# Tokens 0 to 255 of x turned on TensorE instead of by the DMA queue, at the start of a fused attention and token-mixer kernel

## The chip, the cores and the metric

The kernel runs on one core of one Trainium2 chip. The metric is the time of one execution on the device in microseconds (us), the median over several runs; lower is better. The profile shows one such execution: when each instruction of the engines TensorE (PE, with its weight loads as PEld), VectorE (DVE), ScalarE (ACT), GpSimd (POOL) and of the DMA-issuing queues of SyncE and ScalarE (SPq, ACTq) began, how long it took and what released it.

## The reference

The input `x` has 2048 tokens of 448 features. Two branches read it, and a gate for each token mixes them:

```
g = sigmoid((x * gate_w).sum(-1, keepdims=True))
a = _A_ref(x, wq, wk, wv, wo, beta)        # attention in 4 segments of 512 tokens, 16 heads of 28
b = _B_ref(x, w1, b1, w2, b2)              # layernorm, then an MLP over the token axis (2048 -> 1792 -> 2048)
return g * a + (1 - g) * b
```

In `_A_ref`, `q = x @ wq`, `k = x @ wk` and `v = x @ wv` are formed first. Each segment then has causal softmax attention inside it and a read of a running memory `M`, which sums `phi(k)^T v` of the earlier segments; the two are blended by `sigmoid(beta)` and projected by `wo`. `_B_ref` contracts the token axis, so it needs `x` with tokens on the partitions; the projections of `_A_ref` contract the feature axis, so they need `x` turned, with features on the partitions. The change is about how the first half of the first segment gets turned.

## The kernel before

**Two copies of x.** `xh` holds `x` as rows, 16 tiles of 128 tokens, loaded by `load_x` (L533). `xT` holds it turned: four feature chunks `c` of 128 features (chunk 3 begins at feature 320 and overlaps chunk 2, and the matmuls on it use half of its rows) by 2048 tokens. `transpose_x(tc)` (L548) fills the 512 tokens of segment `tc` with two DMAs that transpose while they move: `dtx{tc}_0` for chunks 0 to 2 and `dtx{tc}_1` for chunk 3.

**The start.** SyncE issues, in this order, the two transposing DMAs of segment 0, the loads of `wk` and `wq`, the two of segment 1, and then three of the four loads of `xh`. ScalarE meanwhile issues the gate vector, the four parts of `wv` (L538 and, for the last part, L542), the last part of `wk` and two biases; only then does it load its function table and begin to compute. TensorE runs ten matmuls on constants (`warm`, L664), a small transposition of the gate vector (`gtr`, L879), and then the value projection of token tiles 0 to 3.

**The value projection** of a tile `t` is split by what it needs. `pra{t}` is chunk 0, `prb{t}` chunk 1, `prt{t}` chunk 2 or 3 over all 128 rows. `lot0` and `lot2` take the remaining 64-row halves of chunk 2 or 3 for two tiles at once, side by side in the array. The turned tokens are the weights of these matmuls, `wv` with the gate vector as column 449 is what streams through. Every projection matmul goes through the helper `mm`, so all of them have line 296. After them come the key projections (`pra0_1`, `pra0_2`, `pra0_0`, a `lok` pair, and so on), which need `wk` spread out to 32 columns a head by VectorE's copies `padk`, `padx` (L675); the pair `lok0_2` also needs the first two such copies of `wq` (`padq0`, `padq1`). `cpv` (L857 on ScalarE, L859 on VectorE) moves a value tile out of PSUM, `gt` (L860) its gate column, `cpk` (L773, L775) a key group. `prt7` is the first matmul that reads segment 1 of `xT`. From there on the program goes through scores (L1015), exponentials (L1024, ScalarE), value products (L1045) and the two token-mixer matmuls (again L296), closely interleaved.

**What sets the order.** `ORDER` is a table with a line-up of operation names for each engine; an entry such as `pra0@5` also gives the PSUM bank. `Sched.plan` puts each engine's instructions out in exactly that order, and `finalize` adds the semaphore waits that the recorded reads and writes require. An engine executes its list in order: whatever stands behind a waiting instruction waits as well. The resources `R_xT[tc][k]` say which part of `xT` an operation reads; before the change there are two for each segment, one for each transposing DMA.

Of the kernel before, what the change touches and what calls it, by code (L numbers as in the profile page):

```python
# [324 lines left out]
u1-15 u2-10*4 u3-5*2 u4-0@4 u3-7*2 sc1_1 u5-0@6*2 u2-14 u5-2*2 u2-15 u3-9*6 u5-4 u3-15 u4-1*5 u5-5*2 pv1@7 u4-6*2
sc1_2 u4-8 u5-7*5 u4-9*4 u5-12 pv0@5 u5-13 sc1_3 u4-13*3 u6-0@7*3 u7-0@5 u6-3 u5-14 u6-4*2 u5-15 u6-6 sc1_4 u6-7 u7-1
u6-8*4 u7-2*2 u6-12 u7-4*3 u6-13*3 sc2_0 u7-7*7 pv2@6 u7-14*2 sc2_1 mst0@4 u8-0@6*2 prq2_1@7 prq2_0@5 loq2_0 sc2_2
u8-2*4 prq2_2@4 u8-6*4 prq2_2h@7 loq2_2 mem1 u8-10*2 u9-0@4 u8-12 u9-1*8 u8-13*2 u11-0@5 sc2_3 u9-9*3 pv3@7 u9-12
u8-15 u9-13*2 u11-1 u9-15 u11-2*4 sc2_4 u10-0@7*3 u11-6*6 u13-0@4 u10-3 pv4@6 sc3_0 u10-4*12 u11-12 u13-1 sc3_1
u13-2*3 u11-13*2 u13-5*2 pv5@6 u11-15 prt9@7 u13-7*4 sc3_2 lot8@6 u13-11*2 u12-0@5*5 prt8 u13-13*3 u12-5 sc3_3  # L330
lot10@67 u12-6*3 prt11 u12-9*7 prt10 sc3_4 mst1@7 prk3_1@4 pv6@5 prk3_0@7 lok3_0 sc4_0 prq3_1@6 prq3_0@7 wo0@5 loq3_0
lw0@4 sc4_1 wo1 pv7@6 prk3_2@5 wo3@7 lok3_2@4 lw2@6 sc4_2 wo2 prx3_3 y0-0@5*5 mem2 y0-5*9 prq3_2h@6 prq3_2@4 loq3_2
sc4_3 y1-0@7*7 y2-0@4 y1-7 y2-1 sc4_4 y2-2*2 y1-8 y3-0@6*3 pv8@5 y2-4 y1-9 sc5_0 y2-5*2 y3-3*3 y1-10 y3-6*5 sc5_1
y3-11*3 y1-11*3 y2-7 wo4@5 sc5_2 lw4@7 wo5 y2-8 pv9@6 y2-9*2 sc5_3 y2-11*3 y5-0@5*7 sc5_4 lw6@64 y5-7 pv10@7 wo7
# [4 lines left out]
lw12 lw14 y10-12 y11-12*2 y10-13 wo14 wo15 wo12 y12-0@4*2 wo13 y13-0@7*4 y15-0@5 y13-4*2 y14-0@6*2 y13-6*4 y12-2
y14-2*2 y13-10 y14-4 y12-3*2 y13-11 y12-5*3 y14-5 y15-1 y12-8*3 y14-6*3 y13-12*2 y12-11*3 y14-9*5 y15-2*12 y15-0#1@7  # L340
y15-1#1 y15-2#1 y15-3#1 y15-4#1 y15-5#1 y15-6#1 y15-7#1 y15-8#1 y15-9#1 y15-10#1 y15-11#1 y15-12#1 y15-13#1""",
    "ACT": """
ldwv0 ldgw ldwv1 ldwv2 ldwvb ldwkb ldb1 ldb2 cpv2 cpv0 gt0 gt2 cpv1 gt3 gt1 ek0_0 cpk0_1 cpk0_3 cpq0_3 ek0_1 cpv7 gt7
cpk1_3 cpq1_3 cpk1_2 cpv6 cpq0_2 gt6 cpq0_0 cpq0_2#1 cpq1_1 cpq1_2 cpq0_1 tb eq1_1 cpq1_2#1 exp0_0@2 cpk1_1 cpv5 cpv4
gt5 gt4 exp0_1@3 cpk2_2 cpk2_3 cpk2_1 exp0_2@4 cpk2_0 exp0_3@0 eq1_0 eq1_2 exp0_4@1 ek0_2 gsq0 exp1_0@5 gsq1 gvh1 gth0
exp1_1@6 gsq2 gth1 ek0_3 eq1_3 gsq3 gvh3 exp1_2@0 ek1_0 gth3 gth2 exp1_3@1 gsq4 gsq5 exp1_4@2 ek1_1 gth5 gth4 exp2_0@3
gsq6 gsq7 exp2_1@4 ek1_2 cpq2_1 exp2_2@5 ek1_3 cpq2_0 gth7 cpq2_2#1 gth6 eq2_2 eq2_0 exp2_3@6 gsq8 gsq9 eq2_1 gvh9
exp2_4@0 gth8 gth9 exp3_0@1 ek2_0 gsq10 ek2_1 gvh10 exp3_1@2 gsq11 gth10 exp3_2@3 cpv9 cpv8 gt8 gt9 gth11 exp3_3@4
cpv11 gsq13 gt11 gsq12 cpv10 exp3_4@0 gth12 gt10 cpk3_0 exp4_0@5 eq2_3 cpq3_1 cpq3_0 exp4_1@6 gth13 cpk3_2 exp4_2@7
cpk3_3 ag2 eq3_1 cpq3_3 ag3 ek2_2 exp4_3@1 ek2_3 exp4_4@2 eq3_0 exp5_0@0 eq3_2 exp5_1@3 exp5_2@4 exp5_3@5 ag5 exp5_4@6  # L350
eq3_3 exp6_0@1 ag6 exp6_1@2 exp6_2@7 cpv13 gt13 cpv12 gt12 exp6_3@0 gt15 gt14 exp6_4@3 exp7_0@4 ag9 exp7_1@5 exp7_2@6
exp7_3@1 exp7_4@2 ag11 ag15 ag14 ag12 ag13""",
# [39 lines left out]
def build_kernel(nc, X, WQ, WK, WV, WO, BETA, W1, B1, W2, B2, GW, OUT):  # L392
# [153 lines left out]
    def transpose_x(tc):  # L546
        for k, (c, n) in enumerate(((0, 3), (3, 1))):
            op("SP", lambda e, c=c, n=n: e.dma_start_transpose(  # L548
                xT[:, c : c + n, tc * 512 : tc * 512 + 512], x2[tc * 512 : tc * 512 + 512, C0[c] : C0[c] + 128 * n]),
               writes=[R_xT[tc][k]], name=f"dtx{tc}_{k}", dma=True, cost=1200 * n, nbytes=227000 * n, prio=(-3, -3, -1, 0)[tc])  # L550
# [217 lines left out]

    def do_k(tc, hg, t0=0, n=512):
        ks = kT[:, hg, tc * 512 + t0 : tc * 512 + t0 + n]  # L770

        def out(b):
            op("ACT", lambda e: e.activation(ks, bank(b)[:, 0:n], ACT.Copy),  # L773
               **buse(b), reads=[bres(b)], writes=[R_kTh[hg] if t0 else R_kT[hg][tc]], name=f"cpk{tc}_{hg}",
               cost=act_cost(n), prio=P_BASE, alt=("DVE", lambda e: e.tensor_copy(ks, bank(b)[:, 0:n]), dve_cost(n)))  # L775
# [603 lines left out]
```

## Time and profile before

| | |
|---|---|
| median of 3 runs | 170.5 us (170.43 to 170.8) |
| the profiled execution | 170.1 us, of which the profile's span is 168.3 us |
| instructions in the span | 4931 |
| busy: TensorE, VectorE, ScalarE, GpSimd | 164.0, 136.9, 130.4, 64.5 us |
| DMA | 25.44 MB, mean 151 GB/s |

Busy time is time in which at least one instruction of the engine is under way. Matmuls overlap in the array, so the ends of TensorE's rows are modelled and its busy share is no measure of its peak; its starts are recorded. In a row of the timeline the first number is the start, the second the time that the group covers, and the brackets at the end say how long the engine sat idle before it and what ended that. Times are us from the span's start.

### The profile page before, as it was taken

How to read it: one execution, taken by the hardware profiler on the slowest of the kernel's cores; microseconds unless marked ns; L12 is line 12 of the kernel's file. 1: busy time of each engine (PE TensorE's matmuls, PEld its weight loads, DVE VectorE, ACT ScalarE, POOL GpSimd, SP SyncE). 2: the span in 40 equal slices, each digit the busy share in tenths (PEclk: the TensorE clock that was granted, in tenths of full speed). 3: DMA queues.
4: the chain of work that ended last, by engine and by line, in shares of the span. 5: the costliest groups of instructions: out<-in, count | busy, mean ns of one | idle time of the engine just before them, and what ended most of it. 6: DMA issues, size and time to landing. Idle time of an engine off the chain costs nothing.

```text
span 168.3 us, 4931 instructions
## 1 busy us (share of the span) xinstructions
PE 164.0 (97%) x2017; PEld 77.6 (46%) x2017; DVE 136.9 (81%) x321; ACT 130.4 (77%) x164; POOL 64.5 (38%) x100
## 2 busy tenths in 40 slices
PE   8799999999999999999999999999999999999994
PEld 3234444444554544544453454444454444454553
DVE  0087999877989989999999999999999979695042
ACT  0359999999999997999999998988985798603200
POOL 5000245261442514142177356445838356541000
DMA  6999999886677955994338202328942129730302
GB/s 144 259 225 296 242 236 237 167 220 189 181 158 221 217 101 146 163 213 126 103 108 182 67 2 63 97 77 157 253 126 84 42 63 283 225 117 27 117 27 82
DMA packets 53974, 25.44 MB, mean 151 GB/s; under 512 B 18416, under 2 KB 53712, under 8 KB 53952
## 3 DMA queue, kind: packets, MB, share of 16 engines
q1 hardware_dynamic: 53160, 24.54, 59.2%
q10 hardware_dynamic: 792, 0.58, 1.6%
q8 instruction: 16, 0.26, 0.7%
q14 instruction: 6, 0.05, 0.1%
HBM read 18.82 MB, written 2.36 MB: 126 GB/s over the span
## 4 chain that ended last, share of the span: by engine, by line
PE 94%; DMA 3%; ACTq 1%; POOL 0%; issue 0%; DVE 0%; POOLq 0%
PE t L296 79%; PE t L1015 8%; PE t L1045 5%; DMA t<-in_A_wv_dram 3%; PE t L896 1%; PE t L1118 1%; ACTq L538 1%; ACTq L559 0%; DVE t L1251 0%; POOL t L557 0%; POOL t L633 0%; POOL t L600 0%; PE t L927 0%; POOL t L632 0%; POOL t L628 0%
## 5 line engine op out<-in xcount | busy, mean ns | idle before, releaser
L296 PE MATMUL t<-t 128*32 128x448 bf16 (+8 forms) x1252 | 140.5, 352 | 1.1 <-DMA t<-in_A_wv_dram 1.0
L296 PEld LDWEIGHTS t<-t 128*32 128x32 bf16 (+2 forms) x1252 | 63.0, 97 | 64.3 <-issue 14.2
L1024 ACT ACTIVATE t<-t 128x2048 bf16<-128x2048 f32 x40 | 75.2, 1879 | 6.8 <-PE t L1015 6.2
L1027 POOL TENSOR_SCALAR_AFFINE_SELECT t<-t 128x512 bf16<-128x512 bf16 x64 | 43.5, 691 | 42.5 <-ACT t L1024 39.6
L1082 POOL TENSOR_TENSOR t<-t 128x448 bf16<-128x448 f32 (+2 forms) x13 | 13.3, 1026 | 19.0 <-DVE t L1075 14.4
L1251 DVE SCALAR_TENSOR_TENSOR t<-t 128x448 bf16<-128x448 f32 (+2 forms) x17 | 10.7, 645 | 10.2 <-PE t L296 10.1
L1015 PE MATMUL t<-t 28*128 28x512 bf16 (+3 forms) x256 | 15.8, 301 | 0.0
L1059 DVE STREAM_TRANSPOSE t<-t 128x512 f32<-128x512 f32 x16 | 11.3, 706 | 2.9 <-PE t L1045 2.7
L965 POOL TENSOR_TENSOR t<-t 128x4 f32<-128x4 f32 x4 | 4.2, 1054 | 23.3 <-DVE t L963 21.6
L1157 ACT ACTIVATE t<-t 128x448 bf16<-128x448 f32 x10 | 7.0, 732 | 7.7 <-PE t L296 7.7
L1045 PE MATMUL t<-t 128*32 128x512 bf16 (+3 forms) x256 | 11.5, 299 | 0.0
L1101 DVE STREAM_TRANSPOSE t<-t 128x512 bf16<-128x512 bf16 x16 | 10.9, 690 | 0.0
L1015 PEld LDWEIGHTS t<-t 28*128 28x128 bf16 x256 | 4.4, 92 | 14.0 <-ACT t L1024 7.7
L956 DVE BATCH_NORM_STATS2 t<-t 128x6 f32<-128x448 bf16 x16 | 9.3, 610 | 1.1 <-DMA t<-in_A_x_dram 1.1
L857 ACT ACTIVATE t<-t 128x448 bf16<-128x448 f32 x13 | 6.8, 546 | 4.2 <-PE t L296 4.2
L1220 DVE SCALAR_TENSOR_TENSOR t<-t 128x448 f32<-128x448 f32 x14 | 9.2, 664 | 0.5 <-ACT t L1215 0.4
L1045 PEld LDWEIGHTS t<-t 128*32 128x32 bf16 x256 | 6.7, 97 | 5.3 <-issue 0.4
L1212 ACT ACTIVATE t<-t 128x448 f32<-128x448 f32 x14 | 8.8, 638 | 0.1
L818 ACT ACTIVATE t<-t 128x512 bf16<-128x512 bf16 x12 | 7.6, 635 | 1.4 <-DVE t L775 1.4
L847 DVE SCALAR_TENSOR_TENSOR t<-t 128x512 bf16<-128x512 bf16 x12 | 8.5, 712 | 0.1
L1075 DVE SCALAR_TENSOR_TENSOR t<-t 128x448 f32<-128x448 f32 x12 | 8.4, 698 | 0.0
L1225 DVE SCALAR_TENSOR_TENSOR t<-t 128x448 bf16<-128x448 f32 x14 | 8.4, 614 | 0.0
(76 smaller groups left out, 129.3 us busy)
## 6 DMA issues: line engine op xcount, KB each, us to landing
t<-in_B_w_dram SPq DMA_DIRECT2D x52, 256.0 KB, 3.4
t<-in_A_x_dram SPq DMA_DIRECT2D x4, 448.0 KB, 4.8
out_dram<-t SPq DMA_DIRECT2D x15, 112.0 KB, 1.9
t<-in_B_w_dram SPq DMA_DIRECT2D x8, 128.0 KB, 2.4
t<-in_A_wv_dram ACTq DMA_DIRECT2D x4, 112.0 KB, 4.1
t<-in_A_wq_dram SPq DMA_DIRECT2D x1, 336.0 KB, 5.1
spare_heads<-t SPq DMA_DIRECT2D x8, 32.0 KB
spare_heads<-t SPq DMA_DIRECT2D x16, 16.0 KB
```

The lines of the kernel that those rows point to most:

```text
L296: last = e.matmul(out[q], w[:, q], x, skip_group_check=True, **kw)
L956: op("DVE", lambda e: e.bn_stats(st6[:, t, :], xh[:, t, :]), reads=[R_x[t]], writes=[R_st6[t]], name=f"bns{t}", cost=512, prio=P_PROJ - 10 ...
L1015: last = e.matmul(bank(hl)[:, c0 : c0 + w], kT[r, hg, s * 512 + j * 128 : s * 512 + j * 128 + 128], qT[r, hg, s * 512 + 128 * j : s * 512 ...
L1024: exps.append(op("ACT", lambda e: e.activation(pslot(g), ps[:, 0:4, :], ACT.Exp, scale=SCALE), reads=R_bank[0:4], writes=[g.res], take=g, ...
L1027: op("POOL", lambda e, c0=c0: e.affine_select(pslot(g)[:, :, c0 : c0 + 128], pslot(g)[:, :, c0 : c0 + 128], pattern=[[0, 4], [1, 128]], co ...
L1045: last = e.matmul(bank(cb)[32 * ((hl + hg) % 4) : 32 * ((hl + hg) % 4) + 32, 128 * j : 512], vaug[:, 4 * s + j, 32 * h : 32 * h + 32], psl ...
L1059: dv(lambda e: e.transpose(tt[:, ia, :], bank(cb)[:, 0:512]), [bres(cb)], [R_tt[ia]], "ta", 630, use=(cb,))
L1082: return e.tensor_tensor(dst, part(n3[0]), part(n3[1]), op=ALU.add)
L1101: dv(lambda e: e.transpose(oT[:, hg, s * 512 : s * 512 + 512], o), [R_ob[hg]] + ([R_obx] if hg else []), qres(hg, s), "ot", 635)
L1212: op("ACT", lambda e: e.activation(gg[:, q, :], bank(b)[:, 0:D], ACT.Square, bias=b1s[:, ft : ft + 1], scale=math.sqrt(GC)), **buse(b), re ...
L1220: op("DVE", lambda e: e.scalar_tensor_tensor(gg[:, q, :], gg[:, q, :], 1.0, vh[:, q, :], op0=ALU.add, op1=ALU.mult), reads=[R_gg[q], R_vh[ ...
L1251: op("DVE", lambda e: e.scalar_tensor_tensor(outst[:, p, c0:c1], bank(b)[:, 0 : c1 - c0], omg[:, T : T + 1], ag(T)[:, c0:c1], op0=ALU.mult ...
```

## The change

`transpose_x(0)` turns tokens 256 to 511 only. Tokens 0 to 255 are loaded as rows, by `load_x("SP", 0, 2)`, which is issued behind `dtx0_0` and ahead of `dtx0_1`; the later load `ldx0` of four tiles becomes `ldx2` of two. A new function `turn_x` multiplies the loaded tiles with the identity: eight matmuls of 128 columns, four into PSUM bank 0 (`xt0_0`, chunks 0 and 1 of both tiles), four into bank 1 (`xt0_1`, chunks 2 and 3). One copy each brings a bank to `xT`: `cx0_0` on ScalarE and `cx0_1` on VectorE. `R_xT[0]` now has four entries, for the two copies and the two shorter DMAs, and `xres` picks those that a projection reads. In the order, value tiles 2 and 3 come ahead of 0 and 1; with them the PSUM banks 4 to 7 are given out in another rotation throughout. All other orders are kept.

```diff
@@ ORDER, the beginning of PE, ACT, DVE and SP
-warm gtr@4 warm2 pra0@5 pra1@6 pra2@7 pra3@4 prb3 prb2 prb0 prb1 lot2 lot0 prt1 prt3 prt2 prt0 pra0_1 pra0_2 pra0_0
+warm gtr@4 warm2 xt0_0 xt0_1 pra2@5 pra3@6 prb2 prb3 pra0@7 pra1@4 prb0 prb1 lot2 lot0 prt2 prt3 prt0 prt1 pra0_1
...
@@ build_kernel
-    R_xT = [R(f"xT{t}_", 2) for t in range(4)]
+    R_xT = [R(f"xT{t}_", 4 if t == 0 else 2) for t in range(4)]
+
+    def xres(tc, cs=range(NCT), halves=range(2)):
+        return [R_xT[0][k] for k in sorted({2 * p + c // (2 + p) for p in halves for c in cs})] if tc == 0 else \
+            [R_xT[tc][k] for k in sorted({c // 3 for c in cs})]
...
     def transpose_x(tc):
         for k, (c, n) in enumerate(((0, 3), (3, 1))):
-            op("SP", lambda e, c=c, n=n: e.dma_start_transpose(
-                xT[:, c : c + n, tc * 512 : tc * 512 + 512], x2[tc * 512 : tc * 512 + 512, C0[c] : C0[c] + 128 * n]),
-               writes=[R_xT[tc][k]], name=f"dtx{tc}_{k}", dma=True, cost=1200 * n, nbytes=227000 * n, prio=(-3, -3, -1, 0)[tc])
+            t0 = tc * 512 if tc else 256
+            op("SP", lambda e, c=c, n=n, t0=t0: e.dma_start_transpose(
+                xT[:, c : c + n, t0 : tc * 512 + 512], x2[t0 : tc * 512 + 512, C0[c] : C0[c] + 128 * n]),
+               writes=[R_xT[tc][k if tc else 2 + k]], name=f"dtx{tc}_{k}", dma=True, cost=1200 * n, nbytes=227000 * n, prio=(-3, -3, -1, 0)[tc])
 
     transpose_x(0)
+    load_x("SP", 0, 2)
...
-    load_x("SP", 0, 4)
+    load_x("SP", 2, 2)
...
+    def turn_x():
+        for k in range(2):
+
+            def fn(e, k=k):
+                for c in (2 * k, 2 * k + 1):
+                    for t in range(2):
+                        at = 256 * (c % 2) + 128 * t
+                        last = e.matmul(bank(k)[:, at : at + 128], xh[:, t, C0[c] : C0[c] + 128], ident[:, :],
+                                        start=True, stop=True, skip_group_check=True)
+                return last
+
+            op("PE", fn, reads=R_x[0:2] + [R_ident], writes=[R_bank[k]], name=f"xt0_{k}", mode="f",
+               cost=pe_cost(128, 128, 128, 128), prio=-1)
+
+            def ends(k=k):
+                return xT[:, 2 * k : 2 * k + 2, 0:256], bank(k).rearrange("p (c t) -> p c t", c=2)
+
+            op("ACT", lambda e, ends=ends: e.activation(*ends(), ACT.Copy), reads=[R_bank[k]], writes=[R_xT[0][k]],
+               name=f"cx0_{k}", cost=act_cost(512), prio=-1,
+               alt=("DVE", lambda e, ends=ends: e.tensor_copy(*ends()), dve_cost(512)))
...
+    turn_x()
```

What stands on the engines at the start is shown by three pairs of listings. Each row is a line of the source, an operation, what it writes and reads, and the semaphores that it waits for; `s_dma_u…` is the semaphore of one DMA.

TensorE before, from the first gate matmul to the key projections: `s_dma_u3`, `u4`, `u5`, `u6` are the four parts of `wv`, `u1` and `u2` the two transposing DMAs, `s_DVE` the gate column and later the spread-out `wk`.

```order
L879 MATMUL t<-t 128x3 [waits s_POOL,s_dma_u12]
L880 MATMUL t<-t 128x1
L664 MATMUL t<-const-bfloat16-1.0 128x512
L296 MATMUL t<-t 128x449 [waits s_DVE,s_dma_u3,s_dma_u1]
L296 MATMUL t<-t 128x449 x3
L296 MATMUL t<-t 128x449 [waits s_dma_u4]
L296 MATMUL t<-t 128x449 x3
L296 MATMUL t<-t 128x449 [waits s_dma_u6,s_dma_u5,s_dma_u2]
L296 MATMUL t<-t 128x449 x7
L296 MATMUL t<-t 128x512 [waits s_DVE]
```

TensorE after, the same stretch: `s_dma_u3` is now the load of the first two x tiles, the parts of `wv` are `u4` to `u7`, and `s_ACT` is the copy `cx0_0`.

```order
L671 MATMUL t<-const-bfloat16-1.0 128x512
L684 MATMUL t<-t 128x128 [waits s_dma_u3]
L684 MATMUL t<-t 128x128 x7
L296 MATMUL t<-t 128x449 [waits s_DVE,s_dma_u4,s_dma_u1]
L296 MATMUL t<-t 128x449
L296 MATMUL t<-t 128x449 [waits s_dma_u5]
L296 MATMUL t<-t 128x449
L296 MATMUL t<-t 128x449 [waits s_ACT]
L296 MATMUL t<-t 128x449 x3
L296 MATMUL t<-t 128x449 [waits s_dma_u7,s_dma_u6,s_dma_u2]
L296 MATMUL t<-t 128x449
L296 MATMUL t<-t 128x449 [waits s_DVE]
```

Eight turning matmuls stand ahead of all projections, and four of the eight matmuls on chunks 0 and 1 now stand behind a wait for ScalarE.

ScalarE after, its issues and its first computing instructions (before, the same list without the row of L694, and the table load belongs to `cpv2`):

```order
L547 DMA t<-in_A_wk_dram 128x448
L575 DMA t<-in_B_b_dram 14x128
L577 DMA t<-in_B_b_dram 16x128
L694 ACT_TABLE_LOAD
L694 ACTIVATE t<-t 128x2x256 [waits s_PE]
L886 ACTIVATE t<-t 128x16x28 [waits s_PE] x2
```

The copy `cx0_0` (L694) is the first computing instruction of ScalarE and stands behind eight DMA issues and the table load.

SyncE after, its first issues (before: the two transposing DMAs of 512 tokens, then the weights, then three loads of four tiles):

```order
L554 DMA_TRANSPOSE t<-in_A_x_dram 128x3x256
L538 DMA t<-in_A_x_dram 128x2x448
L554 DMA_TRANSPOSE t<-in_A_x_dram 128x1x256
L543 DMA t<-in_A_wk_dram 128x2x448
L543 DMA t<-in_A_wk_dram 128x448
L543 DMA t<-in_A_wq_dram 128x3x448
L547 DMA t<-in_A_wq_dram 128x448
L554 DMA_TRANSPOSE t<-in_A_x_dram 128x3x512
L554 DMA_TRANSPOSE t<-in_A_x_dram 128x1x512
L538 DMA t<-in_A_x_dram 128x2x448
L538 DMA t<-in_A_x_dram 128x4x448 x2
```

One more issue stands ahead of the weights on this queue, and the two transposing DMAs of segment 0 have half their tokens.

More of the change, by code (lines that the diff above doesn't have):

```diff
@@ L325 @@
[L325 to L334, printed above, removed]
@@ L340 @@
-y14-2*2 y13-10 y14-4 y12-3*2 y13-11 y12-5*3 y14-5 y15-1 y12-8*3 y14-6*3 y13-12*2 y12-11*3 y14-9*5 y15-2*12 y15-0#1@7
+warm gtr@4 warm2 xt0_0 xt0_1 pra2@5 pra3@6 prb2 prb3 pra0@7 pra1@4 prb0 prb1 lot2 lot0 prt2 prt3 prt0 prt1 pra0_1
+pra0_2 pra0_0 btr@7 lok0_0 lok0_2 prk0_0 prx0_3 prk0_2 prk0_1 prt7@5 prx1_3@6 prk1_2@4 lot6@7 lok1_2 loq0_0 loq0_2
+prq0_2 prq0_0 prt6 prq1_2@5 prq0_2h prq1_1@6 prq1_2h@4 loq1_0@7 loq1_2 prq0_1 prq1_0 prk1_1@6 sc0_0 lok1_0@5 lot4@74
+prk1_0 prt5 prt4 sc0_1 prk2_1@6 prx2_3@5 prk2_2@4 lok2_2 lok2_0@7 sc0_2 prk2_0 u1-0@4*5 u0-0@6 u1-5 u0-1*2 u2-0@5*3
@@ L350 @@
[L350 to L352 removed]
+ldwv0 ldgw ldwv1 ldwv2 ldwvb ldwkb ldb1 ldb2 cx0_0 cpv2 cpv0 gt0 gt2 cpv1 gt3 gt1 ek0_0 cpk0_1 cpk0_3 cpq0_3 ek0_1
+cpv7 gt7 cpk1_3 cpq1_3 cpk1_2 cpv6 cpq0_2 gt6 cpq0_0 cpq0_2#1 cpq1_1 cpq1_2 cpq0_1 tb eq1_1 cpq1_2#1 exp0_0@2 cpk1_1
@@ L353 @@
+exp4_2@7 cpk3_3 ag2 eq3_1 cpq3_3 ag3 ek2_2 exp4_3@1 ek2_3 exp4_4@2 eq3_0 exp5_0@0 eq3_2 exp5_1@3 exp5_2@4 exp5_3@5 ag5
+exp5_4@6 eq3_3 exp6_0@1 ag6 exp6_1@2 exp6_2@7 cpv13 gt13 cpv12 gt12 exp6_3@0 gt15 gt14 exp6_4@3 exp7_0@4 ag9 exp7_1@5
+exp7_2@6 exp7_3@1 exp7_4@2 ag11 ag15 ag14 ag12 ag13""",
     "DVE": """
-ob0 gw padk0 padx0 cpv3 padk1 padx1 padk2 padx2 padq0 padq1 b2c padq2 b1c padq3 cpk0_0 cpk0_2 mk0_0 bns3 bns1 bns0
-phk0_0 bns2 bna1 bna3 bna2 bns7 bns9 bna0 bns5 bns10 vpe0 bns11 bns6 bna9 cpq1_0 bna7 bns4 bna6 gcol0 bna5 bna4 vpe4
@@ L356 @@
-nmr0 bna10 bns8 ln1 b1h ln2 bna8 cpk1_0 b1s mk0_1 bns13 bna11 phk0_1 nmr4 bns15 ln0 bna15 omgh vpe8 ln3 ln4 gh ln5
-cpq2_3 bns12 bna12 bna13 bns14 ln6 mq1_1 bna14 nmr8 ln11 ln8 ln9 vpe12 ln10 ln7 omg0 nmr12 mg0 ln12 ln13 ln15 ln14
+ob0 gw cx0_1 padk0 padx0 cpv3 padk1 padx1 padk2 padx2 padq0 padq1 b2c padq2 b1c padq3 cpk0_0 cpk0_2 mk0_0 bns3 bns1
+bns0 phk0_0 bns2 bna1 bna3 bna2 bns7 bns9 bna0 bns5 bns10 vpe0 bns11 bns6 bna9 cpq1_0 bna7 bns4 bna6 gcol0 bna5 bna4
+vpe4 nmr0 bna10 bns8 ln1 b1h ln2 bna8 cpk1_0 b1s mk0_1 bns13 bna11 phk0_1 nmr4 bns15 ln0 bna15 omgh vpe8 ln3 ln4 gh
@@ L762, in proj_d @@
         ts = slice(tc * 512 + t0, tc * 512 + t0 + n)
-        need = R_xT[tc]
+        need = xres(tc)
         return dict(n=n, w=lambda c, rows: wqk[rows, c, 4 * G : 4 * G + 4, :].rearrange("p h j -> p (h j)"),
                     x=lambda c, rows: xT[rows, c, ts], need=need + R_w, use=xuse(tc).get("use", ()),
-                    by=lambda c: [need[c // 3]] + [R_w[k] for k in range(len(R_w)) if R_w[k] not in R_wkp or k % 3 == (0, 0, 1, 2)[c]],
+                    by=lambda c: xres(tc, (c,)) + [R_w[k] for k in range(len(R_w)) if R_w[k] not in R_wkp or k % 3 == (0, 0, 1, 2)[c]],
                     name=name + ("h" if t0 else ""), out=out)
@@ L778, in do_k @@
         if tc == 0:
-            P["first"] = [((0, 1), [R_xT[0][0], R_wkp[0], R_wkp[3]])]
+            P["first"] = [((0, 1), xres(0, (0, 1)) + [R_wkp[0], R_wkp[3]])]
         return P
@@ L861, in out, with rx @@
                **buse(b), reads=[bres(b)], writes=[R_gth[t]], name=f"gt{t}", cost=60, prio=P_BASE)
-        rx = R_xT[t // 4]
+        def rx(cs=range(NCT)):
+            return xres(t // 4, cs, (t % 4 // 2,))
         P = dict(n=D + 1, w=lambda c, rows: xT[rows, c, t * 128 : t * 128 + 128],
-                 x=lambda c, rows: wvx[rows, c, 0 : D + 1], need=rx + R_wv + [R_gw],
-                 by=lambda c: [rx[c // 3], R_wv[c], R_gw],
+                 x=lambda c, rows: wvx[rows, c, 0 : D + 1], need=rx() + R_wv + [R_gw],
+                 by=lambda c: rx((c,)) + [R_wv[c], R_gw],
                  use=xuse(t // 4).get("use", ()), name=f"prt{t}", out=out)
         if t < 4:
-            P["first"] = [((0,), [rx[0], R_wv[0], R_gw]), ((1,), [R_wv[1]])]
+            P["first"] = [((0,), rx((0,)) + [R_wv[0], R_gw]), ((1,), rx((1,)) + [R_wv[1]])]
         return P
```

55 lines of the change are left out of this document (31 added, 24 removed).

## The prediction

> **What bounds the kernel now.** I read the page first: the busy times, and the chain of work that ended last by engine.
>
> ```profile
> PE 164.0 (97%) x2017; PEld 77.6 (46%) x2017; DVE 136.9 (81%) x321; ACT 130.4 (77%) x164; POOL 64.5 (38%) x100
> PE 94%; DMA 3%; ACTq 1%; POOL 0%; issue 0%; DVE 0%; POOLq 0%
> ```
>
> TensorE carries 94% of the chain, DMA 3%. Where the DMA part lies is told by the chain in order of time (start, duration, what), and whether TensorE ever pauses later by the busy times of stretches (PE, then weight loads, DVE, ACT, POOL).
>
> ```profile
> 2.34 0.56 ACTq L538
> 2.90 0.03 issue
> 2.93 4.36 DMA t<-in_A_wv_dram
> 7.29 0.14 issue
> 7.43 2.78 PE t L296 x14
> ```
>
> ```profile
> 0.00:7.43 7.43, 5.50 (x21) 2.02 (x21) 0.45 (x2) 1.28 (x1) 2.20 (x15) 1.00 0.85 182
> 7.43:20.00 12.57, 12.57 (x74) 5.48 (x75) 9.95 (x32) 9.61 (x25) 0.54 (x1) 1.00 1.06 258
> 20.00:60.00 40.00, 40.00 (x522) 18.70 (x521) 36.41 (x104) 39.02 (x50) 16.81 (x25) 1.00 0.87 203
> ```
>
> The DMA part is the last quarter of `wv`, landing at 2.93 + 4.36 = 7.29 us, and from 7.43 on TensorE is never without work. So this change can matter in one way only: by when TensorE gets through the value projections and into the unbroken part. Whatever that moment moves by, the end moves by about as much. The timeline of that stretch, with TensorE's weight loads (PEld) as the sharper clock:
>
> ```profile
> 4.56 0.51 PEld L296 LDWEIGHTS t<-t 128*128 128x128 bf16 x4 [0.39 <-DMA t<-in_A_x_dram]
> 4.59 0.92 PE L296 MATMUL t<-t 128*128 128x449 bf16 x4
> ...
> 5.12 1.28 ACT L857 ACT_TABLE_LOAD   x1 [5.12 <-issue]
> ...
> 5.90 0.49 PEld L296 LDWEIGHTS t<-t 128*128 128x128 bf16 x4 [0.84 <-DMA t<-in_A_wv_dram]
> 5.91 0.93 PE L296 MATMUL t<-t 128*128 128x449 bf16 x4 [0.40 <-DMA t<-in_A_wv_dram]
> 7.40 0.14 PEld L296 LDWEIGHTS t<-t 64*128 64x128 bf16 x4 [1.00 <-DMA t<-in_A_x_dram]
> 7.43 2.78 PE L296 MATMUL t<-t 64*128 64x449 bf16 x14 [0.59 <-DMA t<-in_A_wv_dram]
> 7.91 0.49 PEld L296 LDWEIGHTS t<-t 128*128 128x128 bf16 x4 [0.37 <-issue]
> 8.22 0.47 DVE L675 COPY t<-t 128x784 bf16<-128x784 bf16 x2 [3.77 <-DMA t<-in_A_wk_dram]
> ...
> 8.70 0.98 ACT L857 ACTIVATE t<-t 128x448 bf16<-128x448 f32 x2 [2.30 <-PE t L296]
> 8.73 0.98 PEld L296 LDWEIGHTS t<-t 128*128 128x128 bf16 x6 [0.33 <-DVE t L675]
> ...
> 10.14 0.11 PEld L296 LDWEIGHTS t<-t 64*128 64x128 bf16 x2
> ...
> 10.19 0.30 DVE L675 COPY t<-t 128x224 bf16<-128x224 bf16 x2 [0.46 <-DMA t<-in_A_wq_dram]
> ...
> 10.54 0.10 PEld L296 LDWEIGHTS t<-t 64*128 64x128 bf16 x2 [0.30 <-DVE t L675]
> 10.86 0.98 PEld L296 LDWEIGHTS t<-t 128*128 128x128 bf16 x6 [0.23 <-issue]
> ...
> 12.11 1.60 PEld L296 LDWEIGHTS t<-t 128*128 128x128 bf16 x9 [0.27 <-issue]
> ...
> 12.56 0.58 ACT L773 ACTIVATE t<-t 128x512 bf16<-128x512 f32 x1
> ```
>
> The four `pra` run from 4.59, the four `prb` from 5.91, when the second quarter of `wv` is there, `lot2` from 7.43, the four `prt` behind it, and the first key matmuls from 8.73. TensorE's waits are visible: before 5.91, before 7.43, a little before 8.73 and before 10.54. All eight matmuls on chunks 0 and 1 are done in the holes ahead of 7.43, where they cost nothing. A 449-column matmul takes (0.92 - 0.35)/3 = 0.19 us from start to start (the last one's own 0.35 is the tail of the modelled end), a 512-column one (12.11 - 10.86)/6 = 0.21.
>
> **The change part by part.**
>
> *The new wait.* In the changed kernel `pra0`, `pra1`, `prb0`, `prb1` read what `cx0_0` has copied on ScalarE. That copy is ScalarE's first computing instruction, behind its eight issues and the table load. The row above has the table load at 5.12, straight behind the last issue; nothing in the change shortens that list, so it ends at 5.12 + 1.28 = 6.40 again. The copy has the shape of L773, 0.58 us: 6.98. From a copy's end to the weight load that waited for it the padding row gives 8.73 - (8.22 + 0.47) = 0.04, and 0.03 more to the matmul: `pra0` starts at about **7.05**. Queued behind it on TensorE is everything else.
>
> *What that moves.* Four matmuls of 0.19 that used to run in the holes now run behind 7.05: 7.81. Then comes the turn from full to half rows; `lot2` and `lot0` take 7.91 - 7.40 = 0.51 for two steps of 0.19, so about 0.1 goes into a turn. `lot2` starts at about 7.91 instead of 7.43: **+0.48**.
>
> *What swallows part of it.* Behind `lot2`, before: `prt` from 7.91, four steps to 8.67, but weights at 8.73 because `padx0` ended at 8.69; a wait of 0.06. And 10.14 to 10.86 is 0.72 for two steps of 0.21 and a turn of 0.1, so 0.2 of waiting, for `padq1` at 10.19 + 0.30 = 10.49. Delayed by 0.48, TensorE meets both as done, if the weights land no later than now. 0.48 - 0.06 - 0.17 (the lower of my readings of that wait) = **+0.25**, with 0.05 either way from the turns.
>
> *The weights' landings* hang on the DMA queues. SyncE's issues and landings, by line (minimum/median/maximum ns, first and last start) and by load:
>
> ```profile
> 0.79 2.67 SPq L548 DMA_TRANSPOSE t<-in_A_x_dram  x2
> 3.51 1.08 SPq L538 DMA_DIRECT2D t<-in_A_wk_dram  x2
> ```
>
> ```profile
> L548 SPq DMA_TRANSPOSE t<-in_A_x_dram x8: 1183/1314/4785, 0.8 to 71.5; - x8
> ```
>
> ```profile
> L538 SPq DMA_DIRECT2D t<-in_A_wk_dram x2: 452/514/577, 3.5 to 4.1; - x2
> L542 ACTq DMA_DIRECT2D t<-in_A_wk_dram x1: 640/640/640, 3.6 to 3.6; - x1
> ...
> DMA to landing us min/median/max: 4.4/4.4/4.7
> ```
>
> ```profile
> L538 ACTq DMA_DIRECT2D t<-in_A_wv_dram x3: 352/380/561, 0.8 to 2.3; - x3
> L542 ACTq DMA_DIRECT2D t<-in_A_wv_dram x1: 607/607/607, 2.9 to 2.9; - x1
> ...
> DMA to landing us min/median/max: 2.1/4.1/4.4
> ```
>
> A transposing issue of one chunk (the 1183 is such a one) is hardly shorter than one of three, so I keep 1.3 for the halved ones, and everything behind them on SPq is issued 0.5 us later, by the added load. Against this stand the bytes: the two DMAs lose 256 KB, the load brings 224 KB forward that came later, so what lies ahead of the weights is about equal. Between these I take landings from 0.5 later to 1 us earlier. `wk` may land at 8.22 + 0.5 before `padk0` delays the delayed TensorE, so it costs nothing.
>
> *The load of two tiles* has no row of its own. Issued at about 2.2 it lands between 2.2 + 2.1 = 4.3 (the first part of `wv`, the least hindered of the plain loads) and 2.2 + 4.7 = 6.9 (the first of `wk`, behind two transpositions). I take 5.1, as only one halved transposition stands ahead of it. The nearest row for the eight turning matmuls is the one group of the same shape:
>
> ```profile
> L296 PE MATMUL t<-t 128*128 128x128 bf16 x14 | 0.9, 219 | 0.0
> ```
>
> 8 x 0.9/14 = 0.5 us, to 5.6, then `pra2`, `pra3`, `prb2`, `prb3` to 6.4: all inside the wait for `cx0_0`, so eight matmuls and a landing up to about 5.7 cost nothing. `cx0_1` on VectorE, 3.77 us idle there before 8.22, is hidden too. Other PSUM banks and the other order of `prt` change no duration.
>
> *Gains elsewhere:* shorter transpositions free DMA time, but no wait of TensorE behind 10.9 is left for it to remove.
>
> Sum: 170.1 + 0.25 = 170.35 for an execution like the profiled one, which lies 0.4 below the median of 170.5. On the median: **170.8** with the rounding up that the turns allow. For this kernel 0.2% (0.34 us) is about what a measurement can tell from no change, so the forecast lies just inside.
>
> **The rivals.**
>
> *Faster: ScalarE is free earlier.* Its issues of equal loads range from 0.35 to 0.64 us. If the longer ones were long because SyncE's transposing issues ran beside them, and the halved ones let go sooner, five issues could save 0.2 each: table load at 4.3, `cx0_0` done at 6.2, `lot2` at 7.1, and with `wk` and `wq` half a microsecond earlier `lok0_2` at 10.1: -0.4, 170.1. It decides when `cx0_0` ends before 6.7. Against it: SyncE issues as long as before, with one more.
>
> *Slower: the load of x lands late.* Past 5.7 every further delay goes one for one into `pra2` and what follows. At 6.6 that is +0.9 on top: 171.7. For it: plain loads issued between 2 and 4 us took 3.9 and more.
>
> *Slower: the copy can't begin at the table load's end.* Before, ScalarE's first activation stood at 8.70, 2.30 behind the load's end, waiting for TensorE, so anything up to 2.3 us may be hidden there. With half of it, 1.15, the end is 171.9. [...]
>
> *Slower: TensorE's clock falls back* in the longer hole up to 7.05. The first constants' weight loads come 0.43 us apart, against 0.21 later:
>
> ```profile
> 2.48 0.15 PEld L664 LDWEIGHTS t<-const-bfloat16-1.0 128*128 128x128 bf16 x1 [0.28 <-issue]
> ...
> 2.91 0.15 PEld L664 LDWEIGHTS t<-const-bfloat16-1.0 128*128 128x128 bf16 x1 [0.27 <-issue]
> ```
>
> The slow stretch lasted some 2.5 us; again at half speed from 7.05 it would cost about 1.3: 172. The holes before did not bring it back, and the new one (6.4 to 7.05, or 5.9 to 7.05 with an early load) is of the same kind.
>
> **How the numbers follow.** Forecast 0.56, with a range of 170.5 to 171.1, split by the bound at 170.84 into 0.32 same and 0.24 slower. ScalarE earlier 0.18: 0.12 faster, 0.06 same. Late load 0.14, late first copy 0.09, clock 0.03: all slower. Together: faster 0.12, same 0.38, slower 0.50. The range leaves out the far end of the late cases and the best of the early one: 170.1 to 171.9.
>
> **What would show it.** In the changed profile: the first activation (L694) within 0.1 us of the table load's end, and `pra0`, the fifth 449-column matmul, about 0.65 us after that; `lot2` near 7.9; no wait for VectorE's copies before the key matmuls; matmul steps of 0.19 and 0.21 throughout. The prediction fails if the turning matmuls begin after 5.7, if the table load has moved from 5.1, or if a pause appears on TensorE behind 11 us.

## The result, and the profile after

| | median us | range us | executions |
|---|---|---|---|
| before | 170.55 | 170.32 to 170.84 | 20 |
| after | 171.24 | 170.54 to 172.81 | 20 |

The ratio after to before is 1.0067, with an interval of 1.0047 to 1.0086: slower, by more than the scatter of the times. The ratios of this text lie near the quotients of the means (here 1.0064), not of the medians (here 1.0040), and leave out an execution that lies more than 1.5% above the fastest of its kernel. The median hides something. The 20 times of the changed kernel lie in two groups with nothing between them: 11 from 170.54 to 171.26 (median 170.91) and 9 from 172.30 to 172.81 (median 172.61), 1.7 us apart. The kernel before has one group. The profiled execution of the changed kernel (170.55, span 168.8) belongs to the lower group.

Its page, the busy times and the chain by engine:

```profile
PE 163.6 (97%) x2020; PEld 78.2 (46%) x2025; DVE 137.4 (81%) x322; ACT 131.1 (78%) x165; POOL 64.2 (38%) x100
PE 91%; ACT 3%; DMA 2%; SPq 1%; issue 0%; DVE 0%
```

The bound is the same: TensorE, with a little DMA ahead of it. ScalarE's busy time is up by 0.7 and VectorE's by 0.5, the two copies. The chain in order of time (start, duration, what) names another transfer than before:

```profile
0.79 1.32 SPq L554
...
2.17 3.88 DMA t<-in_A_x_dram
...
6.09 0.62 PE t L684 x8
6.71 4.17 PE t L296 x22
```

Before, the head of the chain was the last quarter of `wv`, landing at 7.29. Now it is the load of the two x tiles: issued at 2.17, behind the first transposing issue of 1.32 us, and landed 3.88 us later, at 6.05. The turning matmuls begin at 6.09, and from there to 20 us TensorE stands still for 0.05 us in all. The timeline of that stretch (start, extent, engine, line, operation, count, and in brackets the idle time ahead and what ended it):

```profile
3.71 0.10 PEld L671 LDWEIGHTS t<-const-bfloat16-1.0 128*128 128x128 bf16 x1 [0.21 <-issue]
3.92 0.10 PEld L910 LDWEIGHTS t<-t 128*128 128x128 bf16 x1
...
4.19 0.38 PE L671 MATMUL t<-const-bfloat16-1.0 128*128 128x512 bf16 x1
...
5.12 1.28 ACT L694 ACT_TABLE_LOAD   x1 [5.12 <-issue]
6.09 0.45 PEld L684 LDWEIGHTS t<-t 128*128 128x128 bf16 x8 [1.82 <-DMA t<-in_A_x_dram]
6.09 0.62 PE L684 MATMUL t<-t 128*128 128x128 bf16 x8 [1.52 <-DMA t<-in_A_x_dram]
6.50 1.30 PEld L296 LDWEIGHTS t<-t 128*128 128x128 bf16 x8
6.53 0.60 ACT L694 ACTIVATE t<-t 128x512 bf16<-128x512 f32 x1
...
8.16 0.11 PEld L296 LDWEIGHTS t<-t 64*128 64x128 bf16 x4 [0.37 <-issue]
8.26 0.47 DVE L704 COPY t<-t 128x784 bf16<-128x784 bf16 x2 [0.82 <-DMA t<-in_A_wk_dram]
...
12.67 0.69 DVE L804 CAST t<-t 128x512 bf16<-128x512 f32 x1 [0.17 <-PE t L296]
```

Three readings. TensorE stands still for 1.5 us, from the end of the second warm-up (4.57) to 6.09, and it waits for the DMA of x. The four matmuls that read what `cx0_0` has copied (`pra0`, `pra1`, `prb0`, `prb1`) then need no wait for it: the copy ends at 7.13, while TensorE is still busy with the four on tokens 256 to 511, and all eight stand in one unbroken row of weight loads from 6.50. And `lot2` loads its weights at 8.16 instead of 7.40, yet nothing between it and the key projections waits any more for VectorE's padding copies.

The last row is a clock hand for all that follows. It is `cpk0_2`, VectorE's second copy out of a key projection, which starts when TensorE has finished `prk0_2`. Before, the same copy (L775) stood here:

```profile
12.16 0.69 DVE L775 CAST t<-t 128x512 bf16<-128x512 f32 x1 [0.17 <-PE t L296]
```

So the head grew by 12.67 - 12.16 = 0.51, and the execution by 170.55 - 170.1 = 0.45. The experiments' traces, read at the same three places (each is explained below), show that nearly the whole difference always lies ahead of this copy (the one profile left out is told of at the end):

| profiled execution | us | turning starts | `lot2` loads weights | `cpk0_2` starts | us minus `cpk0_2` |
|---|---|---|---|---|---|
| before | 170.10 | none | 7.40 | 12.16 | 157.94 |
| after | 170.55 | 6.09 | 8.16 | 12.67 | 157.88 |
| after_again | 172.39 | 6.43 | 9.96 | 14.46 | 157.93 |
| fill | 171.37 | 6.64 | 8.71 | 13.22 | 158.15 |
| fill_again | 171.31 | 6.71 | 8.78 | 13.29 | 158.02 |
| early | 170.28 | 5.10 | 7.88 | 12.39 | 157.89 |
| order_only | 170.47 | none | 7.53 | 12.31 | 158.16 |
| early_dve_again | 170.14 | 4.90 | 7.56 | 12.07 | 158.07 |
| early_dve_wk | 170.06 | 4.75 | 7.61 | 12.12 | 157.94 |
| act_load_dve | 172.51 | 6.19 | 10.05 | 14.56 | 157.95 |

The last column moves by 0.3 us at most while the times move by 2.4. What the change costs, it costs in the first 15 us.

### The profile page after: what moved, and what is told of

It is laid out like the page before. It is cut to its first block, busy times and chain, and to the rows that moved or that the text cites. A ratio compares the mean times of both kernels' runs of the same rounds, so it can differ in the third digit from the quotient of the medians.

```text
span 168.8 us, 4945 instructions
## 1 busy us (share of the span) xinstructions
PE 163.6 (97%) x2020; PEld 78.2 (46%) x2025; DVE 137.4 (81%) x322; ACT 131.1 (78%) x165; POOL 64.2 (38%) x100
## 4 chain that ended last, share of the span: by engine, by line
PE 91%; ACT 3%; DMA 2%; SPq 1%; issue 0%; DVE 0%
PE t L296 76%; PE t L1046 8%; PE t L1076 5%; DMA t<-in_A_x_dram 2%; ACT t L1055 2%; PE t L927 1%; SPq L554 1%; PE t L1149 1%; ACT t L802 1%; ACT t L886 1%; PE t L684 0%; DVE t L1282 0%; ACT t L889 0%; PE t L958 0%
## 5 line engine op out<-in xcount | busy, mean ns | idle before, releaser
L296 PE MATMUL t<-t 128*32 128x448 bf16 (+9 forms) x1247 | 139.4, 352 | 0.5 <-ACT t L802 0.2
L1249 DVE TENSOR_SCALAR t<-t 128x448 f32<-128x448 f32 x10 | 6.5, 676 | 2.4 <-ACT t L1243 2.3
```

The source lines that it names most:

```text
L296: last = e.matmul(out[q], w[:, q], x, skip_group_check=True, **kw)
```

## The experiments

Two questions were open: what makes two groups, and what the rest of the loss is. Medians and ratios are against the kernel before on the same chip.

### The changed kernel again

No edit.

> The changed kernel once more, unaltered. Its 20 times stand in two groups: 11 from 170.54 to 171.26 us and 9 from 172.30 to 172.81, while those of before lie within 170.32 to 170.84. Theory (clock): in the upper group TensorE's clock is at half speed for a while, because TensorE now pauses in one piece until the load of the first two x tiles lands (6.04 us in the profile); it expects the two groups again, some 40 to 50% in the upper one. Rival (load): in the upper group that load lands 1.7 us later; it expects the same two groups. Rival (chip): the groups belong to that chip or hour; it expects one group of about 171 us.

Measured: 9 executions, three from 170.81 to 170.89 and six from 172.39 to 174.37; median 172.71, ratio 1.01 (1.0061 to 1.0138). The profile fell on an execution of the upper group, 172.39, so the two groups can be laid side by side. Its timeline over the same stretch:

```profile
3.34 0.15 PEld L671 LDWEIGHTS t<-const-bfloat16-1.0 128*128 128x128 bf16 x1 [0.28 <-issue]
3.77 0.15 PEld L671 LDWEIGHTS t<-const-bfloat16-1.0 128*128 128x128 bf16 x1 [0.28 <-issue]
4.20 0.15 PEld L910 LDWEIGHTS t<-t 128*128 128x128 bf16 x1 [0.28 <-DMA t<-in_gate_w_dram]
...
4.71 0.59 PE L671 MATMUL t<-const-bfloat16-1.0 128*128 128x512 bf16 x1
...
6.43 1.03 PE L684 MATMUL t<-t 128*128 128x128 bf16 x8 [1.13 <-DMA t<-in_A_x_dram]
...
8.76 0.15 PEld L296 LDWEIGHTS t<-t 128*128 128x128 bf16 x1 [0.22 <-issue]
9.13 0.15 PEld L296 LDWEIGHTS t<-t 128*128 128x128 bf16 x1 [0.23 <-issue]
9.49 0.10 PEld L296 LDWEIGHTS t<-t 128*128 128x128 bf16 x1 [0.21 <-issue]
9.96 0.11 PEld L296 LDWEIGHTS t<-t 64*128 64x128 bf16 x4 [0.37 <-issue]
```

The steps tell TensorE's rate. The constants come 0.43 apart to the end; in the lower group's execution the loads come 0.21 apart from 3.71 on. The eight turning matmuls cover 1.03 us instead of 0.62. The 449-column matmuls, 0.19 apart in the prediction's rows, come 0.37 apart (8.76, 9.13, 9.49) until about 9.4. TensorE ran at half its rate until then. The load cost this execution 0.34 more (6.43 against 6.09), the rate the rest: `cpk0_2` is at 14.46 instead of 12.67, 1.79 later, so 1.45 for the rate.

When the steps shorten varies from execution to execution: the short step is there from 3.7 on in one and from about 9.4 on in another of the same kernel. The first of these is 2.9 us behind the first matmul (0.82), the second 8.6. The granted clock of the windows view doesn't show it. Here is the head of the kernel run again, up to `cpk0_2` (length, busy times of PE, PEld, DVE, ACT and POOL, granted clock, DMA share, GB/s), half rate and all:

```profile
0.00:14.48 14.48, 12.53 (x53) 5.06 (x54) 4.37 (x18) 3.88 (x10) 2.19 (x15) 1.00 0.88 225
```

The clock column says 1.00. Of the fifteen executions in the upper groups, four list a mean clock of 0.99, the others 0.999 or 1.0. The distance of equal steps is what has to be read.

### The hole filled

If the hole ahead of 6.09 is what keeps the rate down, constants in it must remove the upper group; if the groups come from something else, they stay.

```diff
-    warm_up(1, "warm2", P_PROJ + 0.01, 3500.0)
+    warm_up(7, "warm2", P_PROJ + 0.01, 3500.0)
```

> The second warming piece has 7 matmuls on constants instead of 1, so that TensorE is busy until about 5.7 us; nothing else differs. Clock: the upper group disappears, all executions between 170.5 and 171.3, median about 170.8 to 170.9 (the wait for the load, +0.5 in the profile, stays). Load: the two groups stay as they are, median about 171.2, as the load doesn't depend on TensorE. Rival (TensorE order): the added matmuls push the turning matmuls back by up to 0.2 us if the load lands before 5.7.

> fill once more, unaltered, on whatever chip this runs. Clock: again no execution in an upper group 1.5 us or more above the lowest (fill had 0 of 6, the changed kernel 9 of 20 and 6 of 9). Rival (fill's six were chance): about half of the executions in an upper group of 172.5 or more.

Measured: 171.39 (171.09 to 171.90, 6 executions), ratio 1.0062 (1.0042 to 1.0082), and on another chip 171.58 (171.10 to 171.75, 6 executions), ratio 1.0068 (1.0041 to 1.0094). The times form one group both times. None of 12 executions lies above 171.9, against 9 of 20 and 6 of 9, together 15 of 29, without the filling. The second one's timeline shows the filling at work:

```profile
4.71 1.98 PE L671 MATMUL t<-const-bfloat16-1.0 128*128 128x512 bf16 x7
5.09 0.15 PEld L671 LDWEIGHTS t<-const-bfloat16-1.0 128*128 128x128 bf16 x1 [0.28 <-issue]
5.44 0.76 PEld L671 LDWEIGHTS t<-const-bfloat16-1.0 128*128 128x128 bf16 x4 [0.20 <-issue]
6.70 0.45 PEld L684 LDWEIGHTS t<-t 128*128 128x128 bf16 x8 [0.51 <-DMA t<-in_A_x_dram]
```

At 5.09 the steps are still slow, as in the upper group's execution. From 5.44 on four loads take 0.76 together, the fast step: the rate rises inside the filling, and the turning matmuls find it up (0.45 for eight). In the profiled execution of the upper group TensorE stands still just then, for 1.13 us up to 6.43, and the short step comes about 4 us later, at 9.4.

What is left is the late load. The first filled execution, same chip as the kernel run again:

```profile
6.64 0.62 PE L684 MATMUL t<-t 128*128 128x128 bf16 x8 [0.74 <-DMA t<-in_A_x_dram]
...
8.71 0.11 PEld L296 LDWEIGHTS t<-t 64*128 64x128 bf16 x4 [0.37 <-issue]
...
13.22 0.69 DVE L804 CAST t<-t 128x512 bf16<-128x512 f32 x1 [0.17 <-PE t L296]
```

Everything is at full rate here (eight turning matmuls in 0.62), and against the profile of the changed kernel the start of turning, `lot2` and `cpk0_2` are all 0.55 later (6.64, 8.71, 13.22 against 6.09, 8.16, 12.67). A later load passes to `cpk0_2` one for one. The loads' own view (first row the issue with its duration in ns, second the time to landing), first of the changed kernel, then of the filled one:

```profile
L538 SPq DMA_DIRECT2D t<-in_A_x_dram x1: 567/567/567, 2.2 to 2.2; - x1
...
DMA to landing us min/median/max: 3.9/3.9/3.9
```

```profile
DMA to landing us min/median/max: 4.4/4.4/4.4
```

Between them lie the 4.2 us of the kernel run again; the second filled execution has 4.5. The median of the filled kernel, forecast at 170.8 to 170.9, came out 0.5 to 0.7 higher. It lies 0.98 and 1.26 above that of before on the same chip, the lower groups of the unfilled kernel only 0.36 and 0.43. So the filling took the upper group away and left more than the lower group's loss. The later landings fit that, but why the load lands later there isn't settled: the filling touches no queue.

### The load first

If the late load is the loss, issuing it ahead of the first transposing DMA must take the loss away.

```diff
-dtx0_0 ldx0 dtx0_1 ldwk0@0 ldwk1 ...
+ldx0 dtx0_0 dtx0_1 ldwk0@0 ldwk1 ...
```

> The load of the first two x tiles is issued ahead of the transposing DMAs on SyncE's queue; nothing else differs. Theory (late load): the load lands by about 3.5 to 4.5 us instead of 6.04, the turning matmuls run right behind the warming ones, and ScalarE's copy is next bound by the end of its table load at 6.40: lot2 near 7.9 instead of 8.17 and the end at about +0.25 us to before (170.8 in the lower group). Rival (ScalarE isn't the next bound): lot2 before 7.6 or the end below before's 170.55. Clock: TensorE still pauses, from about 5.6 to 7.05, so an upper group may remain, rarer than in the changed kernel.

Measured: 170.29 (170.25 to 171.03, 11 executions), ratio 0.9999 (0.9987 to 1.0011). One group, and no loss that can be measured. Its timeline:

```profile
5.07 1.28 ACT L694 ACT_TABLE_LOAD   x1 [5.07 <-issue]
5.10 0.94 PE L684 MATMUL t<-t 128*128 128x128 bf16 x8
...
5.90 0.94 PE L296 MATMUL t<-t 128*128 128x449 bf16 x4
...
6.37 0.60 ACT L694 ACTIVATE t<-t 128x512 bf16<-128x512 f32 x1
7.01 0.50 PEld L296 LDWEIGHTS t<-t 128*128 128x128 bf16 x4 [0.62 <-ACT t L694]
...
7.88 0.11 PEld L296 LDWEIGHTS t<-t 64*128 64x128 bf16 x4 [0.37 <-issue]
```

This is the case that the prediction took for the changed kernel. Turning is done in the hole; the copy on ScalarE begins 0.02 us after the table load (5.07 + 1.28 = 6.35, then 6.37); `pra0` waits for it until 7.01, and `lot2` loads at 7.88, as forecast (7.05 and 7.91). The head is 0.23 longer than in the profile before (12.39 against 12.16), near the forecast 0.25, but the medians don't show it. The load landed at about 4.1, but even as the first issue of its queue it took 3.3 us:

```profile
DMA to landing us min/median/max: 3.3/3.3/3.3
```

### The order of tiles and the banks alone

The kernel before, with value tiles 2 and 3 first and the new order of banks, and nothing turned on TensorE.

```diff
-warm gtr@4 warm2 pra0@5 pra1@6 pra2@7 pra3@4 prb3 prb2 prb0 prb1 lot2 lot0 prt1 prt3 prt2 prt0 ...
+warm gtr@4 warm2 pra2@5 pra3@6 prb2 prb3 pra0@7 pra1@4 prb0 prb1 lot2 lot0 prt2 prt3 prt0 prt1 ...
```

> The kernel before with the changed kernel's order of value tiles (2 and 3 first) and its bank rotation, but with all of segment 0 turned by the DMA and no turning matmuls. Theory: the order and the banks cost nothing, within 0.2% of before (170.2 to 170.9), one group. Rival (order): the reordered evacuations or banks make up the +0.5, about 171.0.

Measured: 170.38 (169.72 to 170.88, 12 executions), ratio 0.9995 (0.9982 to 1.0008). Order and banks cost nothing that can be measured; the loss is in how x gets to TensorE.

### The first copy on VectorE

With the load first, `cx0_0` is what holds TensorE, for 0.62 us up to 7.01. VectorE stands idle there for 1.01 us ahead of its own copy at 6.08, and its rows show no table load.

```diff
 ACT
-... ldb1 ldb2 cx0_0 cpv2 cpv0 ...
+... ldb1 ldb2 cpv2 cpv0 ...
 DVE
-ob0 gw cx0_1 padk0 ...
+ob0 gw cx0_0 cx0_1 padk0 ...
 SP
-dtx0_0 ldx0 dtx0_1 ldwk0@0 ...
+ldx0 dtx0_0 dtx0_1 ldwk0@0 ...
```

> The load of the first two x tiles first on SyncE's queue, as in early, and both copies of the turned tokens on VectorE, so that neither waits for ScalarE's table load. Theory (the table load is the next bound): in early pra0 stands at 7.02 because ScalarE's copy runs from 6.36 to 6.96; on VectorE the first copy ends at about 6.4, pra0 follows prb3 without a wait at 6.7, lot2 comes to about 7.5 instead of 7.88, the first key matmuls to 8.8 (wk lands at 8.25 and its copies end at 8.75), and the end 0.3 us below early: about 170.0 against 170.4 before. Rival (the weights wk bind anyway): key matmuls not before 9.1, no change to early.

> early_dve unaltered, for a profile that can be read (the profiled execution of early_dve ran 325.98 us, alone among 12). Theory (the table load was the next bound): lot2 near 7.5, the first key matmuls near 8.8, prt7 near 12.1 against 12.40 in early, time 170.0 to 170.3. Rival (wk binds): key matmuls at 9.1 as in early.

Measured: 170.23 (169.98 to 170.52 in 11 executions, the profiled twelfth is told of at the end), ratio 0.9994 (0.9978 to 1.001); again, on another chip, 170.10 (169.87 to 170.43, 12 executions), ratio 0.9974 (0.9958 to 0.9989). The timeline of the second:

```profile
4.90 0.61 PE L684 MATMUL t<-t 128*128 128x128 bf16 x8
...
5.32 1.29 DVE L696 CAST t<-t 128x512 bf16<-128x512 f32 x2 [0.29 <-PE t L684]
5.93 1.26 PEld L296 LDWEIGHTS t<-t 128*128 128x128 bf16 x8 [0.60 <-DMA t<-in_A_x_dram]
...
7.56 0.11 PEld L296 LDWEIGHTS t<-t 64*128 64x128 bf16 x4 [0.37 <-DMA t<-in_A_x_dram]
...
8.19 0.47 DVE L704 COPY t<-t 128x784 bf16<-128x784 bf16 x2 [1.57 <-DMA t<-in_A_wk_dram]
...
8.71 1.08 PEld L296 LDWEIGHTS t<-t 128*128 128x128 bf16 x6 [0.16 <-DVE t L704]
```

Both copies are done by 6.61, and no wait on them is left. The forecast held: `lot2` moves from 7.88 to 7.56, the key projections stand at 8.71, and the time is 170.10. TensorE now waits elsewhere: until 5.93 for the first transposing DMA, which stands behind the load on its queue, and before 8.71 for the padding of `wk`, whose landing nothing has moved. This is the best version run: at the most 0.4% faster than before, and in one of its two comparisons not to be told from it.

### The weights ahead of the second transposition

As the version before, with `wk` issued earlier.

```diff
-ldx0 dtx0_0 dtx0_1 ldwk0@0 ldwk1 ...
+ldx0 dtx0_0 ldwk0@0 dtx0_1 ldwk1 ...
```

> As early_dve, and the first half of wk is issued ahead of the last chunk's transposing DMA. If wk binds in early_dve, it lands about 1 us earlier here and the key matmuls follow lot2 and the prt without a wait, another 0.1 to 0.3 us: 169.8. Rival: the transposing DMA, issued 0.6 us later, lands at about 7.6 and holds lot2 back, no gain on early_dve (170.0) or a loss of 0.2.

Measured: 170.51 (170.06 to 171.24, 12 executions), ratio 1.0011 (0.9994 to 1.0029): no gain. The wait changes its owner:

```profile
7.61 0.11 PEld L296 LDWEIGHTS t<-t 64*128 64x128 bf16 x4 [0.67 <-DMA t<-in_A_x_dram]
```

`wk` is there before it is needed (its first copies end at 7.45), and `lot2` now waits for the delayed second transposition, as the rival said. One queue carries both, and in these two profiles whichever goes second is waited for.

### The load on ScalarE's queue

As the version with both copies on VectorE, but with the load issued by ScalarE instead of SyncE, second in its list.

```diff
-    load_x("SP", 0, 2)
+    load_x("ACT", 0, 2)
...
 ACT
-ldwv0 ldgw ldwv1 ldwv2 ldwvb ...
+ldwv0 ldx0 ldgw ldwv1 ldwv2 ldwvb ...
 SP
-dtx0_0 ldx0 dtx0_1 ...
+dtx0_0 dtx0_1 ...
```

> As early_dve, but the load of the first two x tiles is issued on ScalarE's queue between the first part of wv and the gate vector, so that the halved transposing DMA is first on SyncE's queue again. Theory (what made the load late is that its packets come after those of the transposition on its queue): on a queue of its own it lands before 5 us although the transposition runs beside it, and the transposition lands near 4.0 to 4.5 as in the changed kernel; lot2 near 7.4 to 7.6 (the last part of wv is issued 0.4 us later), time 170.0 to 170.3. Rival (the 16 engines serve no plain load while or just after they transpose, whatever the queue): it lands at about 6 again, time about 171.2 or in two groups.

Measured: 172.32 (170.13 to 172.71, 12 executions), ratio 1.0064 (1.0028 to 1.0101), in two groups again: 4 from 170.13 to 170.65 and 8 from 172.19 to 172.71. The profile is of the upper one:

```profile
3.77 0.15 PEld L671 LDWEIGHTS t<-const-bfloat16-1.0 128*128 128x128 bf16 x1 [0.28 <-issue]
5.73 0.11 PEld L910 LDWEIGHTS t<-t 128*128 128x128 bf16 x1 [1.81 <-DMA t<-in_gate_w_dram]
...
8.92 0.15 PEld L296 LDWEIGHTS t<-t 128*128 128x128 bf16 x1 [0.23 <-issue]
9.30 0.15 PEld L296 LDWEIGHTS t<-t 128*128 128x128 bf16 x1 [0.23 <-issue]
10.05 0.11 PEld L296 LDWEIGHTS t<-t 64*128 64x128 bf16 x4 [0.60 <-issue]
```

The load's own view:

```profile
DMA to landing us min/median/max: 4.1/4.1/4.1
```

Issued at 1.20 on ScalarE's queue, the load took 4.1 us, no less than behind the transposition (3.9 to 4.5), and landed at about 5.3. That is neither the forecast (before 5) nor the rival's 6; so the place behind the transposition on SyncE's queue can't be the whole reason that it takes so long. Here it was early enough, but the gate vector `gw` behind it was not: TensorE's next weights wait 1.81 us for it, to 5.73, in the middle of the warm-up. The result is the same pair of groups, with steps of 0.38 (8.92 to 9.30) until after 9.3. So it isn't the load of x as such that makes them. What the two profiles of upper groups share is a pause of TensorE while its constants still come 0.43 apart, there 1.13 us for the load of x, here 0.91 us for the gate vector. In the lower group's profile the steps had gone to 0.21 before its pause of 1.52. (The weights' idle time begins at 3.92; the last constants' matmuls run on until about 4.8, so TensorE itself pauses for 0.91 us.)

## Why the prediction was right, and where it was wrong

The number, 170.8, was 0.44 low, the range held 171.24, and slower was the likeliest of the three signs. But the loss didn't come about as forecast. By the prediction's own sign, turning matmuls that begin after 5.7, its account failed: they begin at 6.09. The wait for ScalarE that made up its +0.25 isn't there, and what is there are two rivals to which it gave 0.17 together, the late load and TensorE's rate. That the number came so near is in part luck: 171.24 is the upper edge of the lower group, which holds 11 of the 20 executions. One more in the upper group would have made it about 171.8, and in the kernel run again, with six of nine in the upper group, the median is 172.71, outside the 170.1 to 171.9.

**The end moves with the head: right.** The time behind `cpk0_2` is 157.9 to 158.2 in all ten profiles. That TensorE is never without work from 7.43 on holds only up to 140 us: of the last 28.3 us of the profile before it is busy for 25.94. That part doesn't move.

**ScalarE's copy sets `pra0`: right as a mechanism, covered in the changed kernel.** Table load at 5.12, copy straight behind it, `pra0` at 7.05, `lot2` at 7.91: with the load on time these are 5.07, 6.37, 7.01 and 7.88. In the changed kernel the copy waited for the turning matmuls instead (6.53) and ended while TensorE was still busy.

**What is swallowed: right.** `lot2` moved by 0.76 in the profile after and `cpk0_2` by 0.51, so 0.25 was swallowed, forecast 0.23; the waits for VectorE's padding copies are gone.

**Turning, `cx0_1`, order and banks cost nothing: right.** Eight turns take 0.45 (0.5 forecast), and order and banks alone give 0.9995.

**The landing of the load, 5.1: the step that failed.** It was taken "as only one halved transposition stands ahead of it", nearer to the first part of `wv` (2.1 us) than to `wk` (4.7). It took 3.9 in the profile after, and 4.2, 4.4 and 4.5 in three others. The nearest rows were the other plain loads issued around that moment: the last quarter of `wv`, issued at 2.93, took 4.36 in the very chain that the prediction quotes. Its late-load rival had this row for it and got 0.14. How much delay is free was right: 5.7 was forecast, and with 2.07 from the start of turning to `lot2`, and 7.88 reached with the load on time, turning may start until 7.88 - 2.07 = 5.81.

What slows the load wasn't taken apart. The profile after, in slices of 0.1 us from 1.5 to 5.5 (busy share of the DMA engines, and what they moved), shows one gap:

```profile
DMA  0007787988999999669992301547899999999999
GB/s 0 0 0 125 152 197 260 322 219 222 219 233 274 269 261 256 117 131 160 170 54 9 18 9 36 72 117 224 314 341 305 359 376 367 385 343 343 374 331 329
```

From 3.5 to 4.0 the engines move 9 to 54 GB/s, with 117 to 170 just ahead of it and over 300 soon behind, and this half microsecond falls into the load's flight. What the DMA engines wait for there stays open. How much of the load's time the gap makes wasn't shown. The 4.1 us on ScalarE's queue and the 3.3 us at the head of SyncE's say that standing behind the transposition is at most part of it.

**"TensorE's clock falls back", 0.03: far too low, and the mechanism was off.** It doesn't fall back: in the profiled execution of the upper group the steps are still 0.43 when the hole begins. The prediction read the rise from one execution, where it came between 3.3 and 3.6, and took it for a fixed point. In other executions the constants are slow to 4.6 and the rise comes later. Three profiles without the hole begin that slowly and reach full rate soon: `order_only` by 5.2, `fill_again` by 5.4, `early` by 5.9. In the kernel run again TensorE stops at 5.30, still slow, and after the hole of 1.13 us stays slow to 9.4. The kernel before has matmuls spread over that time, and none of its 92 executions here lies over 171.37; the changed kernel has a hole of 1.1 to 1.5 us there, and 15 of 29 lie over 172. The price was right: 172 forecast for such an execution, "about 1.3" for the rate, and 1.45 measured.

**The late first copy, 0.09: fallen.** In `early`, where nothing else holds the copy, 0.02 us lie between the end of the table load (1.28 us) and the first activation; the rival took 1.15.

**From the profiled execution to the median: too much.** The sum gave 170.35 for an execution like the profiled one, and 0.4 was added because the median of before lay that much higher. The kernel that fulfilled the sum's conditions has its median at 170.29. Ten of its eleven times lie within 0.21 us, while 26 of the kernel before on that chip spread over 0.99. A likely reason, only argued: the head of that kernel is set by the table load, which hardly moves (it starts at 5.07 to 5.15 in all ten profiles), and that of the kernel before by landings, which do (`lot2`, which waits for them, loads at 7.40 in its profile and at 7.53 in that of `order_only`).

So of the 0.69 us between the medians, order, banks, turning and the wait for ScalarE hold none that can be measured. Both parts come from the load of two x tiles at its place in SyncE's queue: it lands too late for the matmuls behind it, at 6.05 in the profile after, and behind the hole that it leaves the one profile of the upper group has steps of 0.37 instead of 0.19. Of the changed kernel's 29 executions 15 lie in that group, of the 12 with the hole filled none.
